# A state-space scan and a gated feed-forward block in one kernel: three more steps a chunk with hp in seven products, and chunk work moved between VectorE and GpSimd

## The chip, the cores and the metric

The kernel runs on one core of a Trainium2 chip. The metric is the device time of one execution in microseconds; smaller is better. A core has TensorE (PE in the profile, with its weight loads as PEld), VectorE (DVE), ScalarE (ACT), GpSimd (POOL) and the queue that issues most transfers (SP). Each takes its instructions in the order in which they were written; semaphores make one wait for another.

## The reference

Two blocks follow each other. The first is a state-space scan over x (4 sequences, 8 heads, 768 positions, 32 channels) with decays a and B, C of 16 states. The second is a feed-forward block over 3072 tokens of 256 channels, with 2048 hidden ones.

```python
for c in range(nc):                      # chunks of 32 positions in the reference
    cum = np.cumsum(la, axis=-1)
    L = np.exp(cum[..., :, None] - cum[..., None, :]) * causal
    y_intra = ((Cc @ Bc.T) * L) @ xc
    y_inter = (Cc @ state) * np.exp(cum)[..., None]
    y[:, :, sl] = y_intra + y_inter
    state = decay_full * state + sum_j(Bc_j xc_j * decay_from_j)
h = x @ w_in                             # x: y, with sequences and positions as tokens
out = (h * np.cos(h)) @ w_out
```

Everything is float32.

## The kernel before, in words

The work is cut into six chunks (NC) of 128 positions of all four sequences, and each chunk into two units of 64 positions. The feed-forward block of a chunk goes in sixteen steps (NF); step n belongs to chunk c = n // 16 and is f = n mod 16 within it, in the texts "step f of chunk c". A step takes 256 of the hidden channels (one pair j) of one unit (steps 0 to 7 the first, 8 to 15 the second):

- **first** (L662): hp = w_in' yT on TensorE, four products of 256 columns (L672).
- **wind_k, wind_w** (L677, L682): the turns k of hp on ScalarE (L679), then w on VectorE (L685). **gate** (L692): the sine on ScalarE (L694). **gated** (L696): gT = hp times that on VectorE (L699).
- **differ** (L720): three instructions on GpSimd (L724, L726, L727) that form the differences gd of gT.
- **second**, two steps later (LAG): o from gT and w_out. From chunk 1 on this is **seven** (L818): a 2x2 block product in seven products of half size (L848) instead of eight, with the differences gd on one side and those of w_out on the other.

Some steps make hp also in seven products (**first7**, L757): then TensorE has seven products of 128 columns (L772), and ScalarE copies one of them (L779) and VectorE adds the others up (L785, L788, L790, L793). One side reads differences of w_in (L743), the other differences of yT that **differ_y** (L745) makes in four subtractions and additions, numbered 0 to 3; 2 uses 0, and 3 uses 2. The seven products are issued in the order 1, 6, 7, 5, 4, 3, 2; product 6 reads result 2 of differ_y, product 4 result 3. Before the change these steps are 9 to 13 of chunks 2, 3 and 4, and steps 1 to 13 of chunk 5 (`runs`, L1034). For chunks 2 to 4 differ_y runs on GpSimd at steps 4, 5 and 6 for the second unit alone; for chunk 5 on VectorE at step 15 of chunk 4. In such steps the second half of the work on hp is done a step later (`late`).

Between these steps the scan of the next chunk is spread out by hand (`steps`, L1006: which part of chunk c's scan stands at which step). Its parts: **decays** (L387, scans on VectorE of 512 elements), **reach** (L586, the running products of a, on VectorE), **turn** (L594, B and C transposed on VectorE, and in turn2, L603 and L605, two copies of C on ScalarE and C times reach on VectorE), **inner** (L615, products g on TensorE), **weigh** (L477, on VectorE), **state** (L510, the carried states added up, four small instructions on VectorE), and the products y, opened at step 14 (L629) and closed at step 15 (L641), from which ScalarE writes yT of the next chunk (L648). GpSimd also scales B (L393) and adds up the finished units of o (L873), one of four pieces a step; ScalarE copies those out of PSUM first (L860, L861).

The order of the work is the order in which the loop over n (L1114) writes it: within a step first, then the work on hp, the scan's parts in the list `behind` (the first of them before gated, the others after), differ_y, the pieces of the sums, and at the end second and the scan's products. No scheduler changes it.

Of the kernel before, what the change touches and what calls it, by code (L numbers as in the profile page):

```python
# [8 lines left out]
FP32 = mybir.dt.float32  # L9
# [3 lines left out]
ALU = mybir.AluOpType  # L13
# [12 lines left out]
def kernel(  # L26
# [12 lines left out]
    nc = tc.nc  # L39
# [3 lines left out]
    N = B.shape[-1]  # L43
# [25 lines left out]
    def bank(shape, name, tag):  # L69
        return psum.tile(shape, FP32, tag=tag, bufs=2, name=name)  # L70
# [4 lines left out]


    along, blocks = {}, {}
    ones = const.tile([P, P], FP32, name="ones")
    V.memset(ones, 1.0)

    def fill(dst):

# [4 lines left out]
                  start=True, stop=True, skip_group_check=True)  # L87


    a_all = dram.tile([NB, H, S], FP32, name="a_all")  # L90
    a_cut = dram.tile([NB, H, S], FP32, name="a_cut")


# [79 lines left out]
    def load_unit_along(k):  # L173

        for p in range(2):
            for s in range(2):
                nc.sync.dma_start(
                    out=alongs[k][:, 2 * p + s, 1:],
                    in_=a_all[2 * s + p, :, k * W:(k + 1) * W].unsqueeze(1).to_broadcast([H, N, W]))

    def load_along(c, seqs=range(NB)):

        if c >= NC:
            return
        if c not in along:
            along[c] = rows.tile([P, NB, P], FP32, tag="along", bufs=2, name="along")
        for b in seqs:
            s = b // 2
            for qs, rs in turns_of[s]:
                hs = slice(2 * qs.start, 2 * qs.stop)  # L190
                nc.sync.dma_start(
                    out=along[c][rs, b], in_=a_all[b, hs, c * P:(c + 1) * P].unsqueeze(1)
                    .to_broadcast([hs.stop - hs.start, N, P]))


    a0 = const.tile([P, 2, W], FP32, name="a0")
# [1 line left out]
    nc.sync.dma_start(out=a0[0:NB * H],  # L198
                      in_=a[:, :, 0:P].rearrange("b h (k i) -> (b h) k i", k=2))
    ms = [scan.tile([P, 2 * H * W], FP32, tag=f"m{b}", bufs=1, name="m") for b in range(NB)]  # L200
    lead, along1, reach1 = (ms[2][:, i * NB * (W + 1):(i + 1) * NB * (W + 1)]
                            .rearrange("p (b i) -> p b i", b=NB) for i in range(3))
    reachs = {1: reach1, 2: along1, 3: reach1}
    alongs = {k: ms[3][:, (k - 2) * NB * (W + 1):(k - 1) * NB * (W + 1)]
              .rearrange("p (b i) -> p b i", b=NB) for k in (2, 3)}
# [299 lines left out]
    def add_state(k):  # L505

        for s in range(2):
            for p in range(2):
                i = k % 2 * W + W - 1
                V.scalar_tensor_tensor(out=after[k][:, s, p], in0=after[k - 1][:, s, p],  # L510
                                       scalar=reach[k // 2, s][:, p, i:i + 1],
                                       in1=after[k][:, s, p], op0=ALU.mult, op1=ALU.add)

    def finish0(k):

# [60 lines left out]
            return exchange  # L576
        return take, add

    def reaches(c, b):

        s, p = divmod(b, 2)
        if p == 0:
            reach[c, s] = scan.tile([P, 2, P], FP32, tag="reach", name="reach")
        for k in range(2):
            i = slice(k * W, (k + 1) * W)
            V.tensor_tensor_scan(out=reach[c, s][:, p, i], data0=along[c][:, b, i],  # L586
                                 data1=ones[:, 0:W], initial=1.0, op0=ALU.mult, op1=ALU.mult)

    turned, ys = {}, {}

    def turn_blocks(c, s):
        turned[c, s] = t = scan.tile([P, 2, 2, P], FP32, tag="turned", bufs=2, name="turned")
# [4 lines left out]

    def turn2(c, s):

        tp = turned.pop((c, s))  # L600
        cT = scan.tile([P, 2, 2, P], FP32, tag="cT2", bufs=2, name="cT2")
        for t in range(2):
            ACT.activation(cT[:, :, t], tp[:, 1], AF.Copy, scale=slot[:, t:t + 1])  # L603
        rT = scan.tile([P, 2, P], FP32, tag="rT", name="rT")
        V.tensor_tensor(out=rT, in0=tp[:, 1], in1=reach[c, s], op=ALU.mult)  # L605
        part[c, s] = (tp[:, 0], cT, rT)

    def inner2(c):

        g = [pair("g") for _ in range(2)]  # L610
        for k, p, s, q in ((k, p, s, q) for k in range(2) for p in range(2) for s in range(2)
                           for q in range(4)):
            bT, cT, _ = part[c, s]
            r, i = group(q, s), slice(k * W, (k + 1) * W)
            PE.matmul(g[q // 2][s * W:(s + 1) * W, q % 2, (2 * k + p) * P:(2 * k + p + 1) * P]  # L615
                      .rearrange("p (t i) -> p t i", t=2),
                      lhsT=bT[r, p, i], rhs=cT[r, p, :, i], start=True, stop=True,
                      tile_position=(r.start, s * W), skip_group_check=True)
        for k in range(2):
            for q in range(2):  # L620
                gs[2 * c + k, q] = g[q][:, :, 2 * k * P:(2 * k + 2) * P]

    def open2(c):

        ys[c] = y = [pair("y") for _ in range(2)]
        for k, p, s, q in ((k, p, s, q) for k in range(2) for p in range(2) for s in range(2)
                           for q in range(4)):
            r, o_, i = group(q, s), W * (q % 2), (2 * k + p) * W
            PE.matmul(y[s][o_:o_ + W, q // 2, i:i + W], lhsT=after[2 * c + k - 1][r, s, p],  # L629
                      rhs=part[c, s][2][r, p, k * W:(k + 1) * W], start=(k == p == 0), stop=False,  # L630
                      tile_position=(r.start, o_), skip_group_check=True)
        for k in range(2 if c < NC - 1 else 0):
            sums(2 * c + 1 + k, [y[s][:, 0, (2 + k) * P:(3 + k) * P] for s in range(2)], group)
# [311 lines left out]
    weigh0(1)  # L945
    weigh_c(1, of_c)

    la = const.tile([RB, NU, P], FP32, name="la")
    cut = const.tile([RB, NU, P], FP32, name="cut")

    def clip_cut():
        G.tensor_scalar(out=cut, in0=a_in, **clip)
        G.memset(cut[:, :, 0:1], 0.0)
        store_a(a_cut, cut)

    def clip_all():
        G.tensor_scalar(out=la, in0=a_in, **clip)

    def store_a(dst, src):
        nc.sync.dma_start(  # L960
            out=dst.rearrange("(u b) h (c p) -> (b h c) u p", u=NU, p=P), in_=src)


    piece = {n: ("in", (n + 3) // 2) if n % 2 else ("out", n // 2) for n in range(NF)}
# [11 lines left out]
        return [k for k, at in unit_at.items() if at[i] == n]  # L976

    def rest_of_loads():
        store_a(a_all, la)
        load_arow(2)  # L980
        fetch("in", 6)
        for s in range(2):
            load_b(2, s)
        fetch("out", 5)
        for s in range(2):
            load_b(2, s, of=C)
        load_unit_along(2)
        fetch("in", 7)
        for s in range(2):
            load_x(2, s)  # L990
        fetch("out", 6)
        load_arow(3)
        fetch("out", 7)
        for of in (B, C):
            for s in range(2):
                load_b(3, s, of=of)
        load_unit_along(3)
        for s in range(2):
            load_x(3, s)
        for k in (4, 5):  # L1000
            for s in range(2):
                load_b(k, s)

    steps = {c: dict(reach=(5, 6), turn=(6, 7), inner=8, weigh=(9, 10), state=(-NF, 12),  # L1006
                     decays=(8, 11, 13, 14), along=(12, 13)) if c == 2 else
             dict(reach=(1, 2), turn=(3, 4), inner=5, weigh=(6, 7), state=(0, 5),
                  decays=(2, 8, 14, 15), along=(6, 7)) for c in range(2, NC)}
    first_decays = (NF + 1, NF + 2, NF + 3, NF + 4)  # L1010

    def chunks_at(n, what):
# [9 lines left out]
    def decays2(k, p):  # L1022
        decays0(k, p)
        if p == 1:
# [6 lines left out]

    runs = [*(range(NF * c + 9, NF * c + 14) for c in range(2, NC - 1)),  # L1034
            range(NC * NF - 15, NC * NF - 2)]
    sevens = {n: r for r in runs for n in r}
    late, at_ = [], {}

    def first_of_seven(n):

# [3 lines left out]
            at_["m"] = pair("m").rearrange("p b (q m) -> p b q m", m=P)  # L1044
        if n == NC * NF - NJ + LAG + 1:
            at_["hp"] = bank([P, TB], "hp", "o")
        to_ = at_["hp"] if i % 3 == (n > NF * (NC - 1)) else bank([P, TB], "hp", "h")
        if n not in sevens:
            first(n, to_=to_)
            return  # L1050
# [57 lines left out]
    for w in (("out", 3), ("in", 5), ("out", 4)):  # L1108
        fetch(*w)
    add_s, rests_of = first_steps()  # L1110
    for k in (2, 3):
        G.memset(alongs[k][:, :, 0:1], 0.0)
    rest_of_loads()
    for n in range(AHEAD, NC * NF + LAG):  # L1114
        c, f = divmod(n, NF)
        if n < NC * NF:
# [25 lines left out]
                wind_w(n)  # L1142
            if closing:
                take_y(0)
            for e, s in chunks_at(n - 1, "turn"):
                turn2(e, s)
            for k in units_at(n, 2):
                turn_unit(k)
            if n + 1 in piece:
# [8 lines left out]
            if joins:  # L1158
# [1 line left out]

            behind = [lambda at=at: decays2(*at) for at in decays_at(n)]
            weighed = [k for k, p in decays_at(n) if p and k != 5 and k < 2 * NC - 1]
            behind += [lambda k=2 * c - 1 + i: add_state(k) for c, i in chunks_at(n, "state")]
            behind += [lambda c=c, b=2 * s + p: reaches(c, b) for c, s in chunks_at(n, "reach")
                       for p in range(2)]
            behind += [lambda at=at: turn_blocks(*at) for at in chunks_at(n, "turn")]
            behind += [lambda k=k, p=p: decays0(k, p) for k, at in unit_at.items()
                       for p in range(2) if at[0][p] == n]
# [22 lines left out]
            if n == runs[-1][0] - 2:  # L1191
                for i in range(4):
                    differ_y(NC - 1, i, V)
            for i, at in enumerate((4, 5, 6, 6) if 2 <= c < NC - 1 else ()):
                if at == f:
                    differ_y(c, i, G, slice(1, 2))
            if unsummed and (c > 1 or summed[0]):
                unsummed[0](range(summed[0], summed[0] + 1), G)
                summed[0] = (summed[0] + 1) % 4
                if summed[0] == 0:  # L1200
# [72 lines left out]
```

## Time and profile before

| | us |
|---|---|
| median of 3 runs (lowest, highest) | 364.44 (363.73, 365.11) |
| profiled execution | 364.44 |
| its span, first to last instruction | 362.7 |
| VectorE busy | 276.0 |
| ScalarE busy | 184.0 |
| GpSimd busy | 239.7 |

The profile is of one execution. Busy time counts each engine's instructions. The chain of waits follows the work that ended last back to the start and gives each microsecond to an engine and a line. A timeline row has the start, the length, engine, line, what is written from what, how many instructions are merged, and in brackets how long the engine stood idle before and who ended that. L numbers are lines of the kernel before.

### The profile page before, as it was taken

What the parts mean: (1) busy time and instruction counts of PE and PEld (TensorE: products, weight loads), DVE (VectorE), ACT (ScalarE), POOL (GpSimd) and SP (SyncE); (2) the same over time, 40 slices, a digit from 0 to 9 for tenths busy, and PEclk for the clock granted to TensorE, in tenths of its full rate; (3) what the DMA queues carried; (4) which work ended last, traced back from release to release, by engine and by line L of the source; (5) the groups of instructions that cost most, each with busy time, mean ns of one, the idle gap of its engine ahead of it and who ended that gap; (6) DMA issues with size and microseconds to landing.
All of it is one profiled execution on the core that took longest, in us unless ns stands there. A gap on an engine that the chain in (4) does not pass through costs nothing.

```text
span 362.7 us, 10240 instructions
## 1 busy us (share of the span) xinstructions
PE 357.0 (98%) x4070; PEld 326.0 (90%) x4070; DVE 276.0 (76%) x504; ACT 184.0 (51%) x352; POOL 239.7 (66%) x387
## 2 busy tenths in 40 slices
PE   8999999999999999999999999999999999999995
PEld 4788888889999999999989999999999999999995
DVE  7779998488876987878766877875776776688864
ACT  3597656544454346534536533545553544444552
POOL 5567767699666677674786666686666465475572
PEclk9999999999999999999999999999999999999999
DMA  7984997666583429113228202110001001001001
GB/s 138 246 284 141 189 196 122 85 125 98 134 129 58 99 51 135 14 34 76 53 53 119 23 3 75 28 33 11 0 2 31 0 3 33 0 3 29 3 17 44
DMA packets 96624, 26.43 MB, mean 73 GB/s; under 512 B 86624, under 2 KB 92480, under 8 KB 96576
## 3 DMA queue, kind: packets, MB, share of 16 engines
q1 hardware_dynamic: 95328, 25.38, 34.9%
q8 instruction: 32, 0.52, 0.6%
q10 hardware_dynamic: 1248, 0.39, 0.5%
q14 instruction: 16, 0.13, 0.1%
HBM read 22.36 MB, written 3.34 MB: 71 GB/s over the span
## 4 chain that ended last, share of the span: by engine, by line
PE 96%; DMA 2%; DVE 1%; issue 0%; ACT 0%; POOL 0%; DVEq 0%
PE o L848 35%; PE hp L672 33%; PE o L808 8%; PE m L772 7%; PE hp L772 5%; DMA bc<-in_C_dram 2%; PE y L641 2%; PE g L615 1%; PE y L489 1%; PE y L629 1%; PE g L468 1%; PE y L537 1%; PE y L527 1%; PE o L900 0%; PE tp L451 0%
## 5 line engine op out<-in xcount | busy, mean ns | idle before, releaser
L672 PE MATMUL hp<-yT,w_in 128*128 128x256 f32 x544 | 129.6, 382 | 0.1
L672 PEld LDWEIGHTS hp<-yT,w_in 128*128 128x128 f32 x544 | 99.0, 190 | 13.8 <-issue 1.4
L724 POOL TENSOR_TENSOR gd<-gT 128x256 f32<-128x256 f32 x79 | 58.1, 735 | 76.9 <-DVE gT L699 61.8
L694 ACT ACTIVATE w<-w,quarter 128x512 f32<-128x512 f32 x96 | 69.4, 723 | 65.8 <-DVE w L685 65.7
L685 DVE SCALAR_TENSOR_TENSOR w<-hp,k 128x512 f32<-128x512 f32 x96 | 65.8, 686 | 45.4 <-ACT k L679 45.2
L679 ACT ACTIVATE k<-hp 128x512 int32<-128x512 f32 x96 | 57.2, 596 | 68.6 <-PE hp L672 60.3
L699 DVE TENSOR_TENSOR gT<-hp,w 128x512 f32<-128x512 f32 x96 | 65.6, 683 | 12.2 <-ACT w L694 8.3
L848 PE MATMUL o<-words,gd 128*128 128x128 f32 x474 | 66.0, 275 | 0.0
L848 PEld LDWEIGHTS o<-words,gd 128*128 128x128 f32 x474 | 59.4, 192 | 0.0
L848 PE MATMUL o<-w_out,gT 128*128 128x128 f32 x316 | 50.4, 278 | 0.0
L848 PEld LDWEIGHTS o<-w_out,gT 128*128 128x128 f32 x316 | 45.4, 191 | 3.1
L726 POOL TENSOR_TENSOR gd<-gT,gd 128x128 f32<-128x128 f32 x79 | 39.6, 501 | 6.2
L727 POOL TENSOR_TENSOR gd<-gT,gd 128x128 f32<-128x128 f32 x79 | 39.0, 493 | 6.2
L848 PE MATMUL o<-w_out,gd 128*128 128x128 f32 x158 | 30.6, 276 | 0.0
L848 PE MATMUL o<-words,gT 128*128 128x128 f32 x158 | 30.6, 275 | 0.0
L808 PE MATMUL o<-w_out,gT 128*128 128x256 f32 x128 | 30.0, 380 | 0.0
L387 DVE TENSOR_TENSOR_SCAN lam<-arow,unit 128x512 f32<-128x512 f32 x20 | 29.9, 1496 | 0.1
L808 PEld LDWEIGHTS o<-w_out,gT 128*128 128x128 f32 x128 | 24.2, 190 | 3.6 <-POOL w_out L283 0.4
L848 PEld LDWEIGHTS o<-words,gT 128*128 128x128 f32 x158 | 24.0, 192 | 0.0
L848 PEld LDWEIGHTS o<-w_out,gd 128*128 128x128 f32 x158 | 24.0, 192 | 0.0
L772 PE MATMUL m<-m,words 128*128 128x128 f32 x168 | 23.4, 276 | 0.0
L772 PE MATMUL hp<-yT,w_in 128*128 128x128 f32 x112 | 21.7, 275 | 0.0
(130 smaller groups left out, 463.6 us busy)
## 6 DMA issues: line engine op xcount, KB each, us to landing
words<-in_moe_w_in_dram SPq DMA_DIRECT2D x8, 512.0 KB
words<-in_moe_w_out_dram SPq DMA_DIRECT2D x8, 512.0 KB
xr<-in_x_dram SPq DMA_DIRECT2D x24, 128.0 KB
arow<-a_cut SPq DMA_DIRECT2D x10, 256.0 KB
arow<-a_cut SPq DMA_DIRECT2D x10, 252.0 KB
out_dram<-sum SPq DMA_DIRECT2D x18, 128.0 KB
bc<-in_B_dram SPq DMA_DIRECT2D x24, 64.0 KB
blocks<-in_B_dram SPq DMA_DIRECT2D x16, 32.0 KB
```

The costliest lines, as they stand in the source:

```text
L387: V.tensor_tensor_scan(out=lams[k][:, p, hs].rearrange(flat), data0=rows_.rearrange(flat), data1=unit0[:, hs].rearrange(flat), initial=0.0 ...
L672: PE.matmul(to_[:, e], lhsT=w_in[:, k, fs], rhs=y[:, k], start=(k == 0), stop=(k == KT - 1), skip_group_check=True)
L679: ACT.activation(k, hp[n], AF.Copy, bias=0.25, scale=INV_2PI)
L685: V.scalar_tensor_tensor(out=w, in0=hp[n], scalar=INV_2PI, in1=k, op0=ALU.mult, op1=ALU.subtract)
L694: ACT.activation(cos, cos, AF.Sin, bias=quarter, scale=TWO_PI)
L699: V.tensor_tensor(out=gT[n], in0=hp.pop(n), in1=cos, op=ALU.mult)
L724: G.tensor_tensor(out=d[:, 0:2], in0=g[:, 1:2].to_broadcast([P, 2, P]), in1=g[:, 3::-3], op=ALU.subtract)
L726: G.tensor_tensor(out=d[:, 2], in0=g[:, 0], in1=d[:, 0], op=ALU.subtract)
L727: G.tensor_tensor(out=d[:, 3], in0=g[:, 2], in1=d[:, 2], op=ALU.subtract)
L772: PE.matmul(dst[q], lhsT=w[q], rhs=y_[q], start=(q in (6, 1, 7)), stop=True, skip_group_check=True)
L808: PE.matmul(o[c, u][:, t], lhsT=g[:, 2 * e + t], rhs=w_out[:, 2 * j + e], start=(j == e == t == 0), stop=(j == NJ - 1 and e == 1), skip_gr ...
L848: PE.matmul(at[q], lhsT=a_[q], rhs=w[q], start=(j == 0 and q in starts), stop=(j == NJ - 1), skip_group_check=True)
```

## The change

- `runs` gets steps 2, 3 and 4 of chunks 2, 3 and 4, so that nine more steps make hp in seven products. In a run of three the second step, not the first and fourth, uses the second bank pair for hp.
- differ_y of chunks 2 to 4 is made for both units, on GpSimd, at steps 0 (results 0 and 1) and 1 (results 2 and 3).
- For chunks 3 to 5 the state additions go to GpSimd (one product with reach, and one addition a step later), at steps 2 and 8 instead of 0 and 5 on VectorE; C times reach goes to GpSimd at steps 6 and 7 (chunk 2 keeps VectorE). One of the decay scans moves from step 2 to step 0, the transposes from steps 3 and 4 to -1 (step 15 of the chunk before) and 1, the copies of C to steps 3 and 4.
- reach becomes one running product for a pair of sequences: two scans of 260 elements a chunk, both at step 5, instead of eight of 64 at steps 1 and 2. For this a_all is stored with a leading zero for each unit, and `lead`, a tile of its own now, restarts the product.
- At steps 2 and 3 of chunks 2 to 5 no piece of a sum is added.

```diff
-    a_all = dram.tile([NB, H, S], FP32, name="a_all")
+    a_all = dram.tile([NB, H, 2 * NC, W + 1], FP32, name="a_all")
...
+    def add_state2(k):
+
+        dec = scan.tile([P, 2, 2, 2 * D], FP32, tag="whole", bufs=1, name="whole")
+        flat = "p s q d -> p (s q) d"
+        G.tensor_tensor(out=dec.rearrange(flat), in0=after[k - 1].rearrange(flat),
+                        in1=reach[k // 2][:, :, k % 2, W:].to_broadcast([P, NB, 2 * D]),
+                        op=ALU.mult)
+        return lambda: G.tensor_tensor(out=after[k], in0=after[k], in1=dec, op=ALU.add)
...
-    def reaches(c, b):
-
-        s, p = divmod(b, 2)
-        if p == 0:
-            reach[c, s] = scan.tile([P, 2, P], FP32, tag="reach", name="reach")
-        for k in range(2):
-            i = slice(k * W, (k + 1) * W)
-            V.tensor_tensor_scan(out=reach[c, s][:, p, i], data0=along[c][:, b, i],
-                                 data1=ones[:, 0:W], initial=1.0, op0=ALU.mult, op1=ALU.mult)
+    def reaches(c, s):
+
+        if s == 0:
+            reach[c] = scan.tile([P, NB, 2, W + 1], FP32, tag="reach", bufs=1, name="reach")
+        V.tensor_tensor_scan(
+            out=reach[c][:, 2 * s:2 * s + 2].rearrange("p b k i -> p (b k i)"),
+            data0=along[c][:, 2 * s:2 * s + 2].rearrange("p b i -> p (b i)"),
+            data1=lead.rearrange("p b i -> p (b i)"), initial=0.0, op0=ALU.mult, op1=ALU.add)
...
+    def scale2(c, s, eng):
+
+        r2[c, s] = rT = scan.tile([P, 2, P], FP32, tag="rT", name="rT")
+        eng.tensor_tensor(out=rT.rearrange("p q (k i) -> p q k i", k=2),
+                          in0=turned.pop((c, s))[:, 1].rearrange("p q (k i) -> p q k i", k=2),
+                          in1=reach[c][:, 2 * s:2 * s + 2, :, 1:], op=ALU.mult)
...
-             dict(reach=(1, 2), turn=(3, 4), inner=5, weigh=(6, 7), state=(0, 5),
-                  decays=(2, 8, 14, 15), along=(6, 7)) for c in range(2, NC)}
+             dict(reach=(5, 5), turn=(-1, 1), cut=(3, 4), scale=(6, 7), inner=5, weigh=(6, 7),
+                  state=(2, 8), decays=(0, 8, 14, 15), along=(6, 7)) for c in range(2, NC)}
...
-    runs = [*(range(NF * c + 9, NF * c + 14) for c in range(2, NC - 1)),
+    runs = [*(range(NF * c + f, NF * c + l) for c in range(2, NC - 1) for f, l in ((2, 5), (9, 14))),
             range(NC * NF - 15, NC * NF - 2)]
...
-            for i, at in enumerate((4, 5, 6, 6) if 2 <= c < NC - 1 else ()):
+            for i, at in enumerate((0, 0, 1, 1) if 2 <= c < NC - 1 else ()):
                 if at == f:
-                    differ_y(c, i, G, slice(1, 2))
-            if unsummed and (c > 1 or summed[0]):
+                    differ_y(c, i, G)
+            for e, s in chunks_at(n, "scale"):
+                if e > 2:
+                    scale2(e, s, G)
+            for add in adds:
+                add()
+            adds[:] = [add_state2(2 * e - 1 + i) for e, i in chunks_at(n, "state") if e > 2]
+            if unsummed and (c > 1 and f not in (2, 3) or summed[0]):
```

## The prediction, made before the changed kernel had run

> **What bounds the kernel now.** I read the page first, for the engine that fills the span; then the chain of waits; then the timelines of four engines side by side where the change puts new work, at the start of a chunk (chunk 3, whose step 0 starts at 191.43).
>
> ```profile
> PE 357.0 (98%) x4070; PEld 326.0 (90%) x4070; DVE 276.0 (76%) x504; ACT 184.0 (51%) x352; POOL 239.7 (66%) x387
> PE 96%; DMA 2%; DVE 1%; issue 0%; ACT 0%; POOL 0%; DVEq 0%
> ```
>
> TensorE is busy for 357.0 of 362.7 us, and 96% of the chain that ended last is its own work. So there are two ways to move the time: fewer TensorE microseconds, or a new gap on TensorE. Time freed or spent elsewhere shows only if it makes or closes such a gap. The table by stretch gives a step's length: first two plain steps, then one step with hp in seven products.
>
> ```profile
> 191.43:194.72 3.29, 3.29 (x24) 3.08 (x23) 1.23 (x3) 1.95 (x7) 2.42 (x5) 1.00 1.08 135
> 194.72:198.01 3.29, 3.29 (x24) 3.08 (x23) 2.24 (x8) 1.32 (x2) 1.64 (x4) 1.00 0.56 85
> 173.50:176.63 3.13, 3.13 (x30) 3.13 (x29) 2.56 (x7) 1.58 (x3) 2.22 (x4) 1.00 0.27 50
> ```
>
> The columns are the stretch, its length, then busy PE, PEld, DVE, ACT and POOL, the granted clock, DMA share and GB/s. The reader is to see that PE is busy for the whole of each: there is no gap to close here, at a clock of 1.00. What can be won is 3.29 - 3.13 = 0.16 us per converted step.
>
> The waits of GpSimd (in all, times, longest) and its and VectorE's timelines at chunk 3, step 0:
>
> ```profile
> POOL gd L724 <- DVE gT L699: 61.8, 60, 2.2
> ```
> ```profile
> 194.49 0.46 POOL L743 TENSOR_TENSOR words<-w_in,words 128x128 f32<-128x128 f32 x1
> 196.44 0.73 POOL L724 TENSOR_TENSOR gd<-gT 128x256 f32<-128x256 f32 x1 [1.50 <-DVE gT L699]
> 197.25 0.46 POOL L726 TENSOR_TENSOR gd<-gT,gd 128x128 f32<-128x128 f32 x1
> 197.78 0.46 POOL L727 TENSOR_TENSOR gd<-gT,gd 128x128 f32<-128x128 f32 x1
> ```
> ```profile
> 194.05 0.69 DVE L685 SCALAR_TENSOR_TENSOR w<-hp,k 128x512 f32<-128x512 f32 x1 [2.06 <-ACT k L679]
> 194.66 0.95 DVE L510 SCALAR_TENSOR_TENSOR state<-state,reach 128x64 f32<-128x64 f32 x4
> 195.60 0.69 DVE L699 TENSOR_TENSOR gT<-hp,w 128x512 f32<-128x512 f32 x1
> ```
> ```profile
> 198.01 1.89 PE L672 MATMUL hp<-yT,w_in 128*128 128x256 f32 x8
> ```
>
> GpSimd is not full, but it waits in order: it sits idle for 1.50 us until VectorE has written gT of step 0, and its three differences of that step end at 198.24. TensorE has started step 2 at 198.01. This order decides my forecast.
>
> **What the change takes away.** Nine steps (2, 3 and 4 of chunks 2, 3 and 4) become seven-product steps: 9 x 0.165 = 1.49 us of TensorE (3.29 against 3.125, the spacing of the o products' starts in the chain at 173.67, 176.79 and 179.92). This is all that can be won, as the plain steps have no gap.
>
> **What it adds on the path.** The sixth product of a run's first step (issued second, after the first) reads the third of the four results of differ_y. In the run at step 9 these are made at steps 4 to 6, long before. For the run at step 2 they are made at steps 0 and 1 on GpSimd, and in the built order they stand behind the three differences of step 0: that is L724, L726, L727 of step 0, differ_y 0 and 1, in chunks 3 and 4 one difference of w_in (L743), differ_y 2 and 3. A queue in order cannot use the 1.50 us of idleness before. So I follow this row through, from the trace's own times, with these prices:
>
> - On VectorE the state addition (0.95 us) that stood between w and gT of step 0 gives way to a decay scan L387, here 1.4 us (rows of 1.22 to 1.45 where GpSimd does little). So gT comes 0.4 to 0.5 us later in chunks 3 and 4. In chunk 2 the state addition took 1.55 us beside GpSimd's work, and the scan meets the same work; I add 0.2 us.
> - From gT's end to L724's start 0.15; L724, L726 and L727 take 1.76 to the next start (196.44 to 198.20).
> - A differ_y of both units is 128x256. The trace has it on GpSimd only at 128x128 (455 ns); L724 and L873 of 128x256 take 0.73 to 0.75 us, with the next start some 0.04 earlier. I take 0.69 spacing, 0.73 for the last. L743 costs 0.42 in chunk 3 and 0.69 in chunk 4. 0.1 us for the signal to TensorE.
>
> Chunk 3: w starts at 194.05, scan 194.66 to 196.05, gT to 196.7, the three differences from 196.85, differ_y 0 at 198.6, 1 at 199.3, L743 at 200.0, differ_y 2 from 200.4 to 201.15, TensorE at 201.25. The product would have been due at 198.01 + 0.22 = 198.23: a gap of 3.0 us. Chunk 2 (step 2 at 141.18, gT ready at 140.3 before, so L724 at 140.46 + 0.2): differ_y 2 ends at 144.5, due 141.40, gap 3.2. Chunk 4 (step 2 at 254.90, w starts at 250.94): scan to 252.95, gT to 253.6, L724 at 253.75, differ_y 0 at 255.5, L743 at 256.9, differ_y 2 to 258.3, due 255.12: gap 3.3. The fourth result, 0.8 after the third, is read by the fourth product issued after it starts 0.67 later: another 0.15 in each. Sum 3.2 + 3.0 + 3.3 + 0.45 = 9.95 us. TensorE has no other work to put into that gap, as its queue is in order too.
>
> Behind the waiting product stand the rest of the seven, the second products of step 0 and all that follows, so the gap is not won back: each later step is as long as TensorE's own work.
>
> **What I cost at nothing, and its cover.** The copies of o (0.46 and 0.59 us on ACT) now come in step 2 behind a 0.26 us copy; the gap covers them, and without it the run at step 9 shows 0.15 us for that place. The cT copies (2 x 0.45) go to steps 3 and 4: ACT has 1.58 there, so 2.5 of 3.13. State additions: VectorE loses 4 x 419 ns twice a chunk; GpSimd gets 2 x 0.73, at steps 2 and 3, 8 and 9, where sums are held back. Step 6 is GpSimd's fullest: 1.76 + rT 0.69 + a sum 0.69 = 3.15 of 3.29. A difference has a slack of about 1.9 us before TensorE reads it; if that cover went, 0.7 a chunk. The products by reach (8 scans of 368 ns in steps 1 and 2) become two scans of 260 in step 5, 1.15 us each by L442: VectorE then has 5.0 us of work in a step of 4.4 (the g products lengthen it) and 2.7 in the next of 3.29, so its lag of 0.6 is gone in one step, against a slack of 1.6 (gT to the hp bank's next use). The transposes move from steps 3 and 4 to -1 and 1; the last load of blocks issues at 190.8 at the latest in chunk 3 and is read from 198.0, which leaves 7 us. Layout of a_all, lead, the dropped fill of ones (0.165 us before the first product waits on DMA): nothing.
>
> **Rules that speak to it.** VectorE writes 128x256 in 433 ns (L790), GpSimd in 735 (L724): 1.7 times. The Trainium skill, GPSIMD Engine Reference, section 4.1 Engine selection, says elementwise work with two inputs belongs on VectorE and is about twice as slow on GpSimd. For the state additions the trace disagrees in effect: four small instructions on VectorE cost 1.68 us, two large ones on GpSimd 1.47. By the page's factor differ_y would be 0.87 us as an estimate, and the total 1.3 us longer.
>
> **The sum.** The profiled execution took 364.44 us (span 362.7 and 1.74 around it), which is also the median of the three. 364.44 - 1.49 + 9.95 = 372.9, rounded to **373.0 us**.
>
> **Rivals.**
>
> - *No gap, not slower* (0.07): if differ_y 2 ends before 198.23 the whole gain stays: 362.95 us, 0.4% faster, which is within what can be told from no change (0.5%). For it: GpSimd is idle for 1.50 us just before, and yT is there from 191.7. Against it: the built order puts the differences of step 0 first, and these alone end at 198.24. It decides if all three subtractions go ahead of L724.
> - *A smaller gap* (0.06): GpSimd overlaps more than the rows show, or gT comes earlier; gaps of 1.5 us each give 364.44 - 1.49 + 4.5 = 367.5.
> - *The gap, and a second one* (0.10): GpSimd at step 6, or the scan and GpSimd hindering each other. At 131.07 a scan L387 took 2.45 us beside a GpSimd instruction, at 186.17 L726 took 1.25 instead of 0.46 beside a scan. With 0.7 a chunk for step 6, or 1.05 more for scans, 374 to 377.
> - *Seven products not shorter here*: 374.4, inside the range, so it has no chance of its own.
>
> **How the numbers follow.** My forecast has 0.77. Low bound: differ_y at GpSimd's shortest 128x256 row (L393, 0.643) and gT no later than now: gaps of 2.8, 2.4 and 2.65, so 364.44 - 1.49 + 7.85 = 370.8; 1.0 less if the 0.15 us stalls in the three runs at step 9 and some restarts (1.92 instead of 1.73) go too: 369.8. High bound: differ_y at L718's 0.956 (2.0 more), the 2.45 us scan in chunk 2 (1.05 more), 376.0; with a part of step 6, 377.0. So 369.8 to 377.0, which leaves out about 0.15. Faster by over 0.5% (below 362.62): 0.02. Within 0.5%: 0.07. Slower by over 0.5% (above 366.26): 0.91.
>
> **What would show it.** In the changed profile the m product of L784 at step 2 of chunks 2, 3 and 4 waits on GpSimd for about 3 us, three times, and the wait table names GpSimd's m (L766) as releaser; GpSimd's differ_y stands behind a difference of gT. Steps 3 and 4 last 3.13. Steps 5 to 8 have no new gap. The forecast is wrong if PE runs through 198 to 202 without a gap, or if a gap stands elsewhere, at step 6 to 8 above all.

## The result and the profile after

The changed kernel takes 377.28 us (median of 6 runs, 376.62 to 378.12), the kernel before 364.34 in the same comparison (6 runs, 363.73 to 365.11): a ratio of 1.036 (95% interval 1.0346 to 1.0374). It is 12.9 us slower; 8.6 were forecast. 377.28 lies just above the range. L numbers from here on are those of the changed kernel: hp L684, its seven products L784, o L860, the differences gd L736, L738, L739, differ_y L766, the differences of w_in L755, gT L711.

The page of the changed kernel, its engines, the row of the granted clock in 40 slices (first that of before), and the chain:

```profile
span 376.3 us, 10363 instructions
PE 361.4 (96%) x4124; PEld 331.5 (88%) x4124; DVE 274.5 (73%) x485; ACT 185.3 (49%) x361; POOL 257.0 (68%) x404
PEclk9999999999999999999999999999999999999999
PEclk9999999999999998999999899999899999999999
PE 70%; SPq 7%; POOL 7%; DVE 6%; DMA 5%; issue 3%; ACT 1%; DVEq 0%; POOLq 0%; ACTq 0%
```

The change was to shorten TensorE's work, yet PE is busy 4.4 us longer (357.0 before), and its share of the chain falls from 96% to 70%. (Not all of these 26% are lost: before a gap the chain follows the work that led to differ_y, beside which TensorE was busy. TensorE stands idle for 14.9 us in all, 5.7 before.) The clock row has three slices at 8, where before has none. So two things happened: TensorE waits, and it is also slower somewhere. The wait table says for what:

```profile
PE m L784 <- POOL m L766: 8.0, 3, 2.7
POOL gd L736 <- DVE gT L711: 65.3, 59, 3.5
```

Three waits of 2.7 us for differ_y: the forecast gap, in its three places. The timelines of TensorE at step 2 of chunk 3, and of VectorE and GpSimd before it:

```profile
202.75 0.39 PE L784 MATMUL hp<-yT,w_in 128*128 128x128 f32 x2
205.80 1.55 PE L784 MATMUL m<-m,words 128*128 128x128 f32 x6 [2.66 <-POOL m L766]
207.15 0.63 PE L784 MATMUL m<-m,w_in 128*128 128x128 f32 x2
...
210.66 0.83 PE L784 MATMUL m<-m,words 128*128 128x128 f32 x6
211.33 0.39 PE L784 MATMUL m<-m,w_in 128*128 128x128 f32 x2
```
```profile
200.69 0.66 DVE L711 TENSOR_TENSOR gT<-hp,w 128x512 f32<-128x512 f32 x1
201.49 0.73 POOL L736 TENSOR_TENSOR gd<-gT 128x256 f32<-128x256 f32 x1 [1.81 <-PE hp L684]
202.29 0.46 POOL L738 TENSOR_TENSOR gd<-gT,gd 128x128 f32<-128x128 f32 x1
202.83 0.46 POOL L739 TENSOR_TENSOR gd<-gT,gd 128x128 f32<-128x128 f32 x1
203.25 1.41 POOL L766 TENSOR_TENSOR m<-yT 128x256 f32<-128x256 f32 x2
204.62 0.46 POOL L755 TENSOR_TENSOR words<-w_in,words 128x128 f32<-128x128 f32 x1
205.03 1.53 POOL L766 TENSOR_TENSOR m<-yT,m 128x256 f32<-128x256 f32 x2
```

GpSimd idles 1.81 us until VectorE has written gT (at 201.35; the row names a TensorE product that ended at the same time), does the three differences, and only then differ_y; TensorE's second product waits until its third result is there. What the forecast did not have is in TensorE's rows: the first six MATMULs after the wait (two for each product here, so products 6, 7 and 5) take 1.55 us, the same six one step later 0.83. The table by stretch (stretch, length, busy PE, PEld, DVE, ACT, POOL, granted clock, DMA share, GB/s) has the reason:

```profile
199.46:202.75 3.29, 3.29 (x24) 3.08 (x23) 2.55 (x5) 1.32 (x2) 1.41 (x3) 1.00 0.93 135
202.75:205.80 3.05, 0.39 (x4) 0.20 (x2) 1.04 (x3) 1.74 (x4) 2.92 (x6) 1.00 0.78 93
205.80:207.15 1.35, 1.35 (x7) 1.35 (x7) 0.00 (x0) 0.00 (x0) 0.73 (x1) 0.56 0.24 54
207.15:208.43 1.28, 1.28 (x8) 1.28 (x7) 0.51 (x2) 0.00 (x0) 0.00 (x0) 0.50 0.39 100
208.43:209.28 0.85, 0.85 (x6) 0.85 (x5) 0.75 (x3) 0.00 (x0) 0.00 (x0) 0.50 0.34 92
209.28:210.44 1.16, 1.16 (x12) 1.16 (x11) 0.69 (x2) 0.00 (x0) 0.53 (x1) 0.96 0.22 52
```

After the wait TensorE has half its clock for 3.41 us (205.95 to 209.36 by the trace's clock record). It is busy, so the loss hides in its busy time. From the product's start to the end of the step are 4.64 us; at full clock it is 3.125 - 0.22 = 2.90.

In the rest of this text, the **rise** at a run's first step is how much longer step 2 lasts than the 3.29 us of before. It is 4.40, 4.40 and 4.34 us in chunks 2, 3 and 4. For chunk 3 that is a gap of 2.83 (product 6 due at 202.97, started at 205.80), plus 1.74 at half clock, less the step's own gain of 0.165. The three gaps are 2.89, 2.83 and 2.78, 8.50 in all; the three losses of clock 1.68, 1.74 and 1.73, 5.15 in all. With the gain of 1.49 and small shifts elsewhere (1.2) that is 8.50 + 5.15 - 1.49 + 1.2 = 13.4; the steps' starts at the end are 13.35 us later in the profiled execution.

### The profile page after: what moved, and what is told of

Its sections match the earlier page's. It is cut to its first block, busy times and chain, and to the rows that moved or that the text cites. A ratio compares the mean times of both kernels' runs of the same rounds, so it can differ in the third digit from the quotient of the medians.

```text
span 376.3 us, 10363 instructions
## 1 busy us (share of the span) xinstructions
PE 361.4 (96%) x4124; PEld 331.5 (88%) x4124; DVE 274.5 (73%) x485; ACT 185.3 (49%) x361; POOL 257.0 (68%) x404
## 4 chain that ended last, share of the span: by engine, by line
PE 70%; SPq 7%; POOL 7%; DVE 6%; DMA 5%; issue 3%; ACT 1%; DVEq 0%; POOLq 0%; ACTq 0%
PE o L860 24%; PE hp L684 19%; PE m L784 10%; PE hp L784 6%; PE o L820 6%; SPq L150 4%; DMA blocks<-in_C_dram 2%; DVE gT L711 2%; POOL gd L736 2%; POOL m L766 2%; DMA arow<-a_cut 1%; POOL gd L738 1%; SPq L107 1%; DMA bc<-in_B_dram 1%; DVE w L697 1%
## 5 line engine op out<-in xcount | busy, mean ns | idle before, releaser
L684 PE MATMUL hp<-yT,w_in 128*128 128x256 f32 x472 | 112.8, 383 | 0.2
L736 POOL TENSOR_TENSOR gd<-gT 128x256 f32<-128x256 f32 x79 | 59.1, 748 | 75.9 <-DVE gT L711 65.3
L684 PEld LDWEIGHTS hp<-yT,w_in 128*128 128x128 f32 x472 | 86.0, 190 | 12.8 <-issue 1.6
L711 DVE TENSOR_TENSOR gT<-hp,w 128x512 f32<-128x512 f32 x96 | 65.7, 684 | 15.2 <-ACT w L706 11.6
L860 PE MATMUL o<-words,gd 128*128 128x128 f32 x474 | 66.4, 276 | 0.3 <-issue 0.2
L860 PEld LDWEIGHTS o<-words,gd 128*128 128x128 f32 x474 | 59.6, 192 | 0.9 <-issue 0.4
L860 PE MATMUL o<-w_out,gT 128*128 128x128 f32 x316 | 51.5, 283 | 0.0
L860 PEld LDWEIGHTS o<-w_out,gT 128*128 128x128 f32 x316 | 45.9, 196 | 2.6
L738 POOL TENSOR_TENSOR gd<-gT,gd 128x128 f32<-128x128 f32 x79 | 41.7, 528 | 6.2
L739 POOL TENSOR_TENSOR gd<-gT,gd 128x128 f32<-128x128 f32 x79 | 37.4, 473 | 6.2
L784 PE MATMUL m<-m,words 128*128 128x128 f32 x222 | 33.2, 289 | 8.0 <-POOL m L766 8.0
L797 DVE TENSOR_TENSOR m<-m 128x128 f32<-128x128 f32 x37 | 10.8, 292 | 36.7 <-PE m L784 33.1
L784 PEld LDWEIGHTS m<-m,words 128*128 128x128 f32 x222 | 29.4, 202 | 8.8 <-POOL m L766 8.6
L387 DVE TENSOR_TENSOR_SCAN lam<-arow,unit 128x512 f32<-128x512 f32 x20 | 31.6, 1582 | 1.7 <-DMA arow<-a_cut 1.7
L860 PE MATMUL o<-w_out,gd 128*128 128x128 f32 x158 | 30.8, 277 | 0.0
L860 PE MATMUL o<-words,gT 128*128 128x128 f32 x158 | 30.5, 275 | 0.0
L791 ACT COPY m<-hp 128x128 f32<-128x128 f32 x37 | 9.7, 262 | 41.5 <-PE hp L784 41.5
L784 PE MATMUL hp<-yT,w_in 128*128 128x128 f32 x148 | 29.4, 281 | 0.0
```

The lines of the kernel that those rows point to most:

```text
L387: V.tensor_tensor_scan(out=lams[k][:, p, hs].rearrange(flat), data0=rows_.rearrange(flat), data1=unit0[:, hs].rearrange(flat), initial=0.0 ...
L684: PE.matmul(to_[:, e], lhsT=w_in[:, k, fs], rhs=y[:, k], start=(k == 0), stop=(k == KT - 1), skip_group_check=True)
L711: V.tensor_tensor(out=gT[n], in0=hp.pop(n), in1=cos, op=ALU.mult)
L736: G.tensor_tensor(out=d[:, 0:2], in0=g[:, 1:2].to_broadcast([P, 2, P]), in1=g[:, 3::-3], op=ALU.subtract)
L738: G.tensor_tensor(out=d[:, 2], in0=g[:, 0], in1=d[:, 0], op=ALU.subtract)
L739: G.tensor_tensor(out=d[:, 3], in0=g[:, 2], in1=d[:, 2], op=ALU.subtract)
```

## The experiments

The theory: the order on GpSimd makes the gap, idleness of TensorE makes the half clock, and together they are the loss. Rivals: the half clock belongs to the place or to the products, not to the idleness; the moved chunk work costs too; the gain of seven products does not arrive here. Each kernel is the changed one with the edit shown, unless it says otherwise, and is compared with the kernel before on the same chip (363.86 to 364.16 us).

| kernel | us | ratio to before (95%) | rise, chunks 2, 3, 4 |
|---|---|---|---|
| changed | 377.28 | 1.036 (1.0346 to 1.0374) | 4.40, 4.40, 4.34 |
| e1_first | 365.08 | 1.004 (1.0025 to 1.0054) | 1.32, -0.17, -0.16 |
| e2_fill | 372.96 | 1.025 (1.0229 to 1.027) | 2.99, 2.79, 2.87 |
| e3_no_run | 363.95 | 0.9997 (0.9988 to 1.0006) | 0, 0, 0 |
| e4_two_first | 371.97 | 1.023 (1.0204 to 1.0256) | 4.49, 1.83, 1.49 |
| e5_one_first | 374.19 | 1.0289 (1.0266 to 1.0312) | 2.98, 3.73, 2.18 |
| e6_first_early | 363.86 | 0.999 (0.9966 to 1.0014) | -0.16, -0.17, -0.17 |
| e7_longer | 383.33 | 1.0536 (1.0523 to 1.055) | 6.05, 6.90, 5.71 |

**e1_first: differ_y ahead of the differences of step 0.** Nothing else is moved.

```diff
+            for i in range(4 if f == 0 and 2 <= c < NC - 1 else 0):
+                differ_y(c, i, G)
...
-            for i, at in enumerate((0, 0, 1, 1) if 2 <= c < NC - 1 else ()):
-                if at == f:
-                    differ_y(c, i, G)
```

> All four differ_y of chunks 2 to 4 are written ahead of the differences of step 0 on GpSimd, still in step 0; nothing else differs from the changed kernel. Theory (TensorE waits for differ_y 2, and after the wait it runs 3 us at half clock): in chunks 3 and 4 result 2 is there about 1 and 2 us before product 6 is due, so no wait and no half clock; in chunk 2 GpSimd is busy without a break before (a 1.55 us difference of w_in, then the differences of step 15 beside a scan), so a wait of about 1.1 us stays. 364 to 366 us, by whether the wait of 1.1 us brings the half clock (1.7 us). Rival (the loss sits in the other moves, or in seven products themselves at steps 2 to 4): 373 us or more, with the products of steps 2 to 4 still slow.

365.08 us: the loss against the kernel before falls from 12.9 to 1.2 us. One wait is left, in chunk 2, and the clock stays at 1.00 behind it:

```profile
142.68 0.94 PE L784 MATMUL m<-m,words 128*128 128x128 f32 x6 [0.99 <-POOL m L766]
143.48 0.49 PE L784 MATMUL m<-m,w_in 128*128 128x128 f32 x2
143.81 0.39 PE L784 MATMUL hp<-yT,words 128*128 128x128 f32 x2
```

So the loss comes from the place of differ_y in GpSimd's queue, and in chunks 3 and 4 the step now takes 3.13 us, as it should.

**e2_fill: TensorE kept busy in the gap.** Twelve more products into the same bank, whose output product 6 overwrites, stand between the run's first and second product.

```diff
-            for q in (1, 6):
-                product(q)
+            product(1)
+            for _ in range(12 if n - 1 not in sevens and f == 2 else 0):
+                PE.matmul(at6, lhsT=w[1], rhs=y_[1], start=True, stop=True, skip_group_check=True)
+            product(6)
```

> The changed kernel, with 12 products of 128 columns (2.7 us of TensorE) put into the wait between products 1 and 6 of the run's first step; they write where product 6 then starts anew, so nothing that is computed changes. Theory (TensorE's clock is halved because it idled): the wait is as long but busy, the clock stays at 1.00, and the 1.7 us a chunk after it go: 377.3 - 5.1 = 372.2 us. Rival (the slow products come from something else in that place, GpSimd's work or transfers): 377 us or more, with a granted clock of 0.5 after the fill as well.

372.96 us. GpSimd's order is as in the changed kernel, and TensorE goes on only when result 2 of differ_y is done: product 6 starts 0.78 us after GpSimd begins results 2 and 3 (first fence, chunk 3), 0.77 us in the changed kernel. But the clock stays (second fence: the stretches around chunk 2's run):

```profile
204.04 1.53 POOL L766 TENSOR_TENSOR m<-yT,m 128x256 f32<-128x256 f32 x2
202.10 2.84 PE L791 MATMUL m<-yT,w_in 128*128 128x128 f32 x24
204.82 0.94 PE L784 MATMUL m<-m,words 128*128 128x128 f32 x6
205.63 0.49 PE L784 MATMUL m<-m,w_in 128*128 128x128 f32 x2
```
```profile
144.00:147.00 3.00, 2.93 (x25) 2.68 (x24) 0.43 (x2) 0.00 (x0) 1.81 (x3) 1.00 0.89 105
147.00:150.00 3.00, 3.00 (x29) 3.00 (x29) 1.85 (x6) 0.76 (x2) 1.28 (x3) 1.00 0.32 80
```

Same place, same products, no idleness: no half clock. That is worth 1.4 to 1.6 us a run in the profiled executions, and the loss against the kernel before falls from 12.9 to 9.1 us. It is the idleness that halves the clock.

**e3_no_run: the moves without the three new runs.** The runs at step 2 are left out; differ_y of both units, the state additions and C times reach on GpSimd, the new scans and transposes all stay.

```diff
-    runs = [*(range(NF * c + f, NF * c + l) for c in range(2, NC - 1) for f, l in ((2, 5), (9, 14))),
+    runs = [*(range(NF * c + f, NF * c + l) for c in range(2, NC - 1) for f, l in ((9, 14),)),
...
-            elif n not in sevens and f not in ((10, 11, 12) if c == 1 else (10, 11)):
+            elif n not in sevens and f not in ((10, 11, 12) if c == 1 else (2, 3, 10, 11)):
```

> The changed kernel without the runs at steps 2 to 4: those nine steps make hp in four products as before, all moves of chunk work stay (differ_y at steps 0 and 1 too, where nobody waits for it until step 9; sums held back at steps 2 and 3). Theory (the moves cost next to nothing): 364.3 to 365.4 us, that is before plus at most the 1.1 us of small shifts that the two traces differ in beside the three waits. Rival (the moves to GpSimd cost as well): 367 us or more.

363.95 us against 363.88. The moved work costs nothing, as the prediction had it. (The copies of o in a run's first step are not in this kernel; e6_first_early below has them.)

**e4_two_first, e5_one_first, e7_longer: other lengths of the gap.** In e4 results 0 and 1 of differ_y go ahead of the differences of step 0, in e5 result 0 alone; in e7 result 1 is made three times, which lengthens the gap.

```diff
+            for i in range(2 if f == 0 and 2 <= c < NC - 1 else 0):      # e5: 1
+                differ_y(c, i, G)
...
-            for i, at in enumerate((0, 0, 1, 1) if 2 <= c < NC - 1 else ()):
+            for i, at in enumerate((-1, -1, 1, 1) if 2 <= c < NC - 1 else ()):      # e5: (-1, 0, 1, 1)
```
```diff
                 if at == f:
+                    for _ in range(2 if i == 1 else 0):      # e7
+                        differ_y(c, i, G)
                     differ_y(c, i, G)
```

> Differ_y 0 and 1 ahead of the differences of step 0, 2 and 3 behind them as in the changed kernel. GpSimd then ends result 2 about 1.4 us later than product 6 is due in chunks 3 and 4; in chunk 2 it has no pause before, so the wait of 2.9 us stays. If a wait of 1.4 us does not halve the clock: 377.3 - 2 x (1.4 + 1.7) = 371.1 us. If any wait does: 374.5 us. Rival (the loss is not in this wait): 377 us.

> Only differ_y 0 ahead of the differences of step 0. By GpSimd's rows the wait should be about 2.1 us in chunks 3 and 4, between the 1.6 us that left the clock at 1.00 and the 2.7 us that halved it; in chunk 2 it stays at 2.7 with the half clock. If 2.1 us halves the clock: 377.3 - 2 x 0.7 = 375.9 us. If not: 377.3 - 2 x (0.7 + 1.5) = 372.9 us.

> The changed kernel with differ_y 1 computed three times instead of once (the same values again), so that the wait is 1.4 us longer in each of the three chunks, about 4.1 us. If the half clock after the wait has a fixed length (3.4 us, 1.5 us lost): 377.3 + 3 x 1.4 = 381.5 us. If it grows with the idle time (1.5 us for 2.7 us): 377.3 + 3 x 2.2 = 383.9 us.

e4 came at 371.97 us, e5 at 374.19, e7 at 383.33. TensorE's waits at the three runs, in the order e4, e5, e7; each fence shows one to three of them:

```profile
144.07 1.14 PE L784 MATMUL m<-m,words 128*128 128x128 f32 x6 [2.74 <-POOL m L766]
...
204.41 0.94 PE L784 MATMUL m<-m,words 128*128 128x128 f32 x6 [1.60 <-POOL m L766]
```
```profile
143.90 0.94 PE L784 MATMUL m<-m,words 128*128 128x128 f32 x6 [2.74 <-POOL m L766]
...
202.84 0.94 PE L784 MATMUL m<-m,words 128*128 128x128 f32 x6 [1.87 <-POOL m L766]
...
204.32 0.64 PE L784 MATMUL hp<-yT,w_in 128*128 128x128 f32 x2
...
263.61 0.94 PE L784 MATMUL m<-m,words 128*128 128x128 f32 x6 [1.94 <-POOL m L766]
```
```profile
208.34 1.65 PE L784 MATMUL m<-m,words 128*128 128x128 f32 x6 [4.11 <-POOL m L766]
```

The stretch that follows in e7:

```profile
208.30:214.03 5.73, 5.69 (x27) 5.70 (x27) 1.95 (x5) 0.00 (x0) 2.06 (x4) 0.50 0.23 58
```

The length of the wait alone does not decide. After 0.99, 1.26, 1.60 and 1.94 us the clock stayed; after 1.87 it was halved, over a microsecond late; after 2.62 to 2.74 it was halved four times out of five, and once, in e5, not at all; after 4.1 to 4.3 always, for 3.0 to 5.7 us of work.

The clock records of the traces show what does. In each trace the clock changes only at instants that lie whole multiples of 3.41 us apart: in the changed kernel it falls at 144.51, 205.95 and 267.39 (18 times 3.41 between them) and is back 3.41 us after each. These are such stretches, four of e5 and one of e4:

```profile
139.20:142.61 3.41, 1.96 (x16) 1.57 (x14) 2.35 (x5) 2.38 (x5) 3.17 (x7) 1.00 0.72 109
142.61:146.02 3.41, 2.12 (x17) 2.06 (x18) 0.68 (x2) 0.00 (x0) 1.96 (x3) 1.00 0.75 94
...
200.64:204.05 3.41, 1.54 (x12) 1.29 (x12) 0.99 (x2) 1.74 (x4) 2.87 (x5) 1.00 0.91 95
204.05:207.46 3.41, 3.41 (x18) 3.41 (x18) 1.95 (x5) 0.00 (x0) 1.12 (x2) 0.50 0.33 81
```
```profile
202.69:206.10 3.41, 1.81 (x16) 1.63 (x14) 1.06 (x3) 1.53 (x4) 2.31 (x5) 1.00 0.94 92
```

What goes with the fall is how long TensorE was busy within one stretch. The wait of 2.74 us in e5 (141.16 to 143.90) is divided by the boundary at 142.61; TensorE is busy for 1.96 and 2.12 us on its two sides, and the clock stays. The wait of 1.87 us lies within one stretch and leaves 1.54 us of work in it; the next is at half clock. After 1.81 (e4, the wait of 1.60) and 1.88 (e5, that of 1.94) the clock stayed, after 0.67 to 0.79 (the four waits of 2.62 to 2.74) it fell, and after 1.73 in e11_shift_less below as well. So the limit in these traces lies between 1.73 and 1.81 us, about half a stretch. This is read from the traces; no run put a wait on either side of a boundary on purpose.

e5 fits neither expectation for that reason: its single executions lie between 373.04 and 375.98 us, and the longer they are, the lower their granted clock (0.995 at 373.04, 0.991 at 374.05 and 374.34, 0.984 at 375.98). e7 came between its two expectations, 381.5 and 383.9, and tells against a loss of fixed size: its three gaps are 4.49, 4.28 and 4.37 us and its losses of clock 1.73, 2.79 and 1.51. In chunk 3, with 2.79, the wait runs on into the first stretch at half clock, TensorE is busy for 2.24 us of it, and the next stretch is at half clock too.

The Trainium skill, TensorE: Matmul & The Clock Gate, Part 1 (The HAM clock gate), states that the clock drops to half after at least one idle window of about 3.4 us, that the window runs freely, and that it takes about 3.4 us of work to come back. The 3.41 us between the changes of clock agree with the length of that window, and the scatter between equal waits with its running freely; the threshold does not hold here, since waits of 2.6 to 2.7 us, and one of 1.87, sufficed.

**e6_first_early: no gap at all.** As e1_first, and the differences of w_in start two steps earlier.

```diff
-        for start, js in zip((2 * NF - 5, 3 * NF - 3, 4 * NF - 3),
+        for start, js in zip((2 * NF - 7, 3 * NF - 3, 4 * NF - 3),
```

> All four differ_y ahead of the differences of step 0, as before in the first experiment, and the four large differences of w_in two steps earlier in chunk 1, so that GpSimd has the time for differ_y in chunk 2 as well. Theory: no wait of TensorE at any of the three places, the clock at 1.00, and the whole gain of the nine steps (1.49 us) comes through but for some tenths of small shifts: 362.6 to 363.3 us, faster than both kernels (before stood at 363.9 in the last comparison). Rival (the earlier differences of w_in delay a difference of gT in chunk 1, and the wait only moves there): 364.5 us or more.

363.86 us, median of 12, and 363.86 before; 362.6 to 363.3 were expected. No wait is left at the three runs, and each saves 0.49 us over its three steps: the 1.49 us arrive. But the starts of the steps lose it again at the ends of the chunks: 0.30 in step 13 of chunk 2, where the weight load of product 6 waits 0.23 us for VectorE (L802), and 0.21, 0.47 and 0.54 in step 15 of chunks 2, 3 and 4, where the small products y stand. In the last two TensorE stops without a releaser:

```profile
246.67 0.94 PE L860 MATMUL o<-words,gd 128*128 128x128 f32 x6 [0.21 <-issue]
...
301.96 0.41 PE L653 MATMUL y<-m,xr 64*32 64x64 f32 x18 [0.35 <-issue]
```

"issue" means that nothing the profile records held it. The work is the same as before the change at that place; what differs is how many instructions TensorE had before it. So a new theory: the stalls go by the position of the instructions in TensorE's stream. The rival is that something of the changed chunk work, unseen, makes them.

**e8_before_shift and e9_first_shift: the position alone.** e8 is the kernel before with 27 tiny products of ones behind its two fills at the start; e9 is e6_first_early with 37 of them. Nobody reads their output.

```diff
-    fill(bank([P, 2, P], "warm", "o"))
+    small = bank([P, 2, P], "warm", "o")
+    fill(small)
+    for _ in range(37):
+        PE.matmul(small[0:32, 0, 0:32], lhsT=nc.const_aps.tensor(1.0, (P, 32), FP32),
+                  rhs=nc.const_aps.tensor(1.0, (P, 32), FP32), start=True, stop=True,
+                  skip_group_check=True)
```

> The kernel before, with 27 small products of ones (32 by 32) at the start whose output nobody reads. They shift all later TensorE instructions by as many as the nine new seven-product steps add. Open is why the kernel with differ_y ahead shows no gain although its three places have no wait any more: in its trace 0.3 to 0.5 us appear at the end of chunks, where TensorE waits for nothing that the profile shows. Theory A (these stalls hang on where the instructions lie in TensorE's stream): such stalls appear here too, 364.5 to 365.5 us. Theory B (they come with the new runs themselves): none, 363.9 to 364.3 us.

> The kernel with differ_y ahead and the differences of w_in two steps earlier, with 37 small products of ones at the start, output read by nobody, so that the later TensorE instructions lie elsewhere in the stream. Theory A: the places of the stalls at the ends of chunks change, and the time moves by some tenths either way, 362.8 to 364.5 us. Theory B: the stalls stay at the same steps, 363.9 us or some tenths more.

e8 came at 373.25 us (ratio 1.0255, 1.0239 to 1.027), far above either expectation, e9 at 364.62 (1.0021, 1.0011 to 1.003), just above its own. e8 has its stalls at the start of the kernel, in products that ran without one before:

```profile
15.77 0.79 PE L468 MATMUL g<-cT,turned 32*64 32x128 f32 x21 [1.07 <-issue]
...
23.69 0.67 PE L537 MATMUL y<-m,xr 64*32 64x64 f32 x27 [4.57 <-issue]
```

Twenty-seven products that do nothing cost 9.3 us there, a stall of 4.57 and half a clock behind it among them. In e9 the stalls at the ends of the chunks are gone:

```profile
246.45 1.65 PE L653 MATMUL y<-m,xr 64*32 64x64 f32 x128
248.03 0.71 PE L860 MATMUL o<-w_out,gT 128*128 128x128 f32 x4
248.58 0.83 PE L860 MATMUL o<-words,gd 128*128 128x128 f32 x6
```

From chunk 2 to the end e9 gains 0.94 us on the kernel before in the profiled execution, where e6 loses 0.2; but its tiny products had cost about 2 us at the start.

**e10_shift_free and e11_shift_less: that position without the cost.** In e10 39 tiny products take the place of both fills, so that what follows stands where it stands in e9; in e11 20 do.

```diff
-    fill(bank([P, 4, P], "warm", "o"))
-    fill(bank([P, 2, P], "warm", "o"))
+    bank([P, 4, P], "warm", "o")
+    small = bank([P, 2, P], "warm", "o")
+    for _ in range(39):      # e11: 20
+        PE.matmul(small[0:32, 0, 0:32], ...)
```

> As e6_first_early, but the two fills of TensorE at the start give way to 39 tiny 32x32 products of ones whose output nobody reads, so that all later instructions lie as far along TensorE's stream as in e9_first_shift. Theory A (the stalls without a releaser go by where the instructions lie): no such stall at the ends of chunks 2 to 4, as in e9_first_shift, and without the 2.2 us that the tiny products took there beside the fills: about 362.4 us, 1.5 below the kernel before. Theory B (the fills also keep the clock up for the first stages): start-up at a lower clock, 364 us or more.

> The same with 20 tiny products in place of the two fills: another place in the stream. Theory A: some of the stalls come back, or fall elsewhere, so a time other than that of e10_shift_free, between 362.5 and 364.5 us. If position means nothing, it is equal to e10_shift_free within 0.3 us.

e10 came at 364.04 us (0.9985, 0.9964 to 1.0007), e11 at 371.61 (1.0195, 1.0164 to 1.0226). e10 has no stall at the chunks' ends and gains 0.9 us from chunk 2 to the end, as expected; the 362.4 did not come, since the second batch of hp products starts at 18.45 (17.67 before), 0.8 us late, half of it by a stall that e9 did not have (first fence). e11 has two larger ones there (second fence), which is more than was expected of any position.

```profile
17.81 0.71 PE L545 MATMUL y<-m,xr 64*32 64x64 f32 x47 [0.41 <-issue]
```
```profile
15.59 0.69 PE L468 MATMUL g<-cT,turned 32*64 32x128 f32 x4 [1.68 <-issue]
...
23.08 0.44 PE L545 MATMUL y<-m,xr 64*32 64x64 f32 x9 [2.79 <-issue]
```

No kernel of this study is measurably faster than the one before.

## Why the prediction was right in its direction and wrong in its size

- **The gap.** Right: the three places, the product, the releaser and the reason (GpSimd's order). Forecast 3.2, 3.0 and 3.3 us, measured 2.89, 2.83 and 2.78. In chunk 2 product 6 started at 144.59 and was forecast for 144.6, but by luck: GpSimd did not wait for gT there (ready at 140.54), it was busy until 140.70 with the differences of the step before, one of which took 1.25 us beside a scan. And step 2 itself began 0.3 later than before. In chunk 4 the decay scan that was put between w and gT of step 0 is not there: VectorE waits 0.86 us for ScalarE and does gT, and the last scan of all (L387, 20 of 512 elements) starts at 255.6 in the step before. That is the 0.5 by which chunk 4 was overestimated. The extra 0.15 for result 3 is hidden by the half clock; in e2_fill, at full clock, product 4 starts 0.81 us after product 6 instead of 0.67. Forecast 9.95, measured 8.50: 1.45 too much.
- **The step that failed** is "so the gap is not won back: each later step is as long as TensorE's own work". The work behind the gap was costed at the clock of the steps before it. It ran at half of that for about 3.4 us in each run: 5.15 us that the sum had no term for. Against the forecast of 8.5 the steps came 13.35 us later: 5.15 and 1.2 (small shifts) too little, less the 1.45 of the gap, which hid part of the miss. The trace of before could hardly have shown it, as TensorE has no long wait there. e2_fill shows idleness as its cause, e1_first that without the gap it is gone.
- **A second gap** was the rival for 374 to 377. There is no second gap in steps 5 to 8; it was the first one that cost more.
- **The gain** of 9 x 0.165 us: right. Steps 3 and 4 take 3.13 us, and in e6_first_early all nine do.
- **What was costed at nothing** (copies, state additions, C times reach, scans, transposes): right, by e3_no_run, and for the copies of o by steps 2 to 4 of e6_first_early; C times reach took 0.99 us on GpSimd instead of 0.69 and still cost nothing. The rows of 128x256 on GpSimd were the right price: two of differ_y take 1.41 us, 0.70 each. The Trainium skill's factor of two (GPSIMD Engine Reference, section 4.1 Engine selection) would have made that 0.87, as an estimate from VectorE's 0.433.
- **The rival of no gap**, 362.95: its condition, all subtractions ahead of the first difference of step 0, was enough in chunks 3 and 4, as e1_first shows, which is that kernel; in chunk 2 a wait of 0.99 us stayed. Its price was not right: 365.08, and 363.86 where that wait goes too (e6). It left out that TensorE loses time at the chunks' ends when its instructions come to stand elsewhere.
- **Small shifts** of 1.2 us were in no term. Of them 0.47 stand in step 15 of chunk 3, where e9 and e10, with other positions, have 0.17 and 0.15. Another 0.30 stand in step 13 of chunk 2, in every kernel with the run at step 2 and not in e3_no_run: it is the wait for L802 named under e6, 0.23 us in the changed kernel too. The rest lies in smaller ones.

## What to carry to other kernels

A new wait on the engine that sets the time is not priced by its length alone: look at the granted clock in the stretch behind it, since a wait of 2.6 to 2.9 us on TensorE cost 1.7 us more there. When work is put on a helper engine whose queue is in order, place it ahead of the instruction that waits for somebody else, not behind it: that alone took the loss from 12.9 to 1.2 us. And a gain below 1% on an engine that is busy all the time has to be read behind the place of the change as well, as small stalls elsewhere can swallow it.

## What the runs showed of the hardware that was not expected

- **Half a clock after a short wait**: 3.41 us of it after 1.87 and 2.62 to 2.74 us of idleness, 6.83 after 4.11, and once none after 2.74. It comes in stretches of 3.41 us, and a fall followed where TensorE had been busy for 1.73 us or less of one.
- **TensorE stalls by position.** The transfers' table of the changed kernel has a queue that brings instructions:

```profile
q8 instruction: 32, 0.52, 0.6%
```

32 packets of 16 KB in all. TensorE has 2 x 4124 products and weight loads, 258 for each packet; e10_shift_free, with 2 x 4198, has 33 packets. In steps of seven products they come about 14.5 us apart (in e6_first_early at 314.6, 329.5 and 343.8). The 128 products y of a chunk's end with their loads are 256 instructions, as many as a packet, in 1.5 us. Each of the seven stalls without a releaser shown above ended 2.3 to 4.0 us after one such packet (in e6_first_early packets at 244.3 and 299.1, stalls until 246.67 and 301.96; in e8_before_shift packets at 12.9 and 21.4, stalls until 15.77 and 23.69). That TensorE there runs through a packet faster than the next one comes is the reading that fits all of them, and the reason why position should matter; it was not tested by a run of its own.
